# Sparse attention that feeds a feed-forward layer, one core: the first batch in another order with fewer instructions, and loads that wait for its first scores

## Chip, cores and metric

The kernel runs on one core of a Trainium2 chip. The metric is the time of one execution in device microseconds (us); the time given is the median of three runs. A page and a trace come from one further execution under the hardware profiler. The engines are named as the profile does: PE (TensorE matmul), PEld (its weight loads), DVE (VectorE), ACT (ScalarE), POOL (GpSimd) and SP (SyncE, which issues loads).

## What is computed

Eight batches of eight heads over 576 tokens with head size 64. The first four heads see the 32 newest keys, the other four the earlier keys of the same residue modulo 32. The heads side by side are the 4608 x 512 input of a feed-forward layer.

```python
scores = np.where(masks[None], scale * np.matmul(q, k.transpose(0, 1, 3, 2)), -1000000000.0)
attn = np.exp(scores - np.max(scores, axis=-1, keepdims=True))
attn = attn / (np.sum(attn, axis=-1, keepdims=True) + 1e-09)
x = np.matmul(attn, v).transpose(0, 2, 1, 3).reshape(B * S, H * D)
h = x @ w_in                                              # 512 -> 2048
g = np.where(h >= 1, h, np.where(h <= -1, 0.0, (h + 1) ** 2 / 4.0))
out = g @ w_out                                           # 2048 -> 512
```

## The kernel before

Attention of a batch is cut in four units: 0 and 1 hold the local heads, 2 and 3 the strided ones. A unit goes through small steps, each with a letter: `s` scores (PE, 96, 48, 48 and 40 small matmuls), the mask (`o` opens both banks with a zero matmul and `i` adds the mask on PE, then `X` and `S` take the maximum and subtract it on DVE straight from PSUM, or ACT copies the scores out with `g`; or `m` adds the mask on DVE), `x` maximum, `a`/`b` subtract, `e` exponential (ACT), `q` sum, `p` sum plus epsilon (ACT), `r` or `w` normalise (POOL or DVE), `f` transposes (PE), `c`/`d` copy them out (ACT, DVE), `v` values (PE), and `h`, `l` (`H`, `M` for tokens past 512) split the result into a rounded and a rest part, `xq_a` and `xq_b`. `0Zs0:17` is 17 zero matmuls into the bank that unit 0's scores will use; they compute nothing that is read.

The feed-forward layer multiplies split operands (three matmuls stand for one). The weights come as packed 64-bit words (`raw`) and are unpacked in five steps, `A` and `L` (ACT), `B` (DVE), `C` (POOL), `D` (ACT, or `g` on DVE) and `E` (DVE); `A0.1` is step A for block 0 of w_out. The first 512 tokens go through 16 up products `h_0` to `h_15`, of which `U` and `V` are the first two; each then has its down products. Later tokens run in larger groups until the end.

The order on every engine is the order in which the program issues, and that is written by hand: `AGENDA` lists the steps with a time in PE units, and the loops take from it what is due. All lines at -66.69 form the head of the program, ahead of the main loops. Loads go out on SP in program order. `load_w(0, 0, after)` makes ACT copy one element of `after` into the buffer of the first weights (`raw_0`), so SP issues that load, and all loads behind it, only after this copy; before, `after` is an element of `qk_1`, the second q and k load.

Of the kernel before, what the change touches and what calls it, by code (L numbers as in the profile page):

```python
# [28 lines left out]
-66.69 B0.1 L0.1  # L29
-63.035 A3.1 C0.1 A4.0 A1.1  # L30
-59.845 L3.0 C3.0 B1.1 D0.1 L1.1 C1.1 1m0 E0.1 1x0 1a0
-59.035 W6
-55.845 D3.0 E3.0 L5.0 L2.1 A5.0 B5.0 C5.0 B4.0
-54.19 L4.0 C4.0 D1.1 E1.1
-53.5 L3.1
-52.5 Z 1s1 1m1 B3.1
-51.845 L7.1 A2.1 B2.1 D4.0 E4.0
# [251 lines left out]
def tile_sparse_attention_then_ffn(  # L289
# [85 lines left out]

    ident_b = const.tile([P, P], BF16, name="ident_b")
    make_identity(nc, ident_b)
    zeros = const.tile([P, P], BF16, name="zeros")
    nc.vector.memset(zeros, 0.0)

# [102 lines left out]
    def whole(raw):  # L483
        return raw[:, :, 1].bitcast(F32).rearrange("p (h e) -> p h e", e=HF)
# [4 lines left out]
        for raw, to in words(f, i):  # L489
            copy(to[:, :, 0], whole(raw))  # L490

    def conv_e(f, i):
        for raw, to in words(f, i):
            nc.vector.tensor_tensor(out=to[:, :, 1], in0=whole(raw), in1=to[:, :, 0].bitcast(F32), op=ALU.subtract)

    def blocks(i, j):
        return wt[i, j].bitcast(F32).rearrange("p a b x e -> p (a b) x e")
# [28 lines left out]
    def ship_sums(i, j):  # L526
        nc.scalar.dma_start(kept[i][j][1], sums.pop((i, j)))

    loaded = {}

    def load_qk(b, p):
        src = qk_l[b, p] if p < 2 else qk_s[b, p - 2]
# [38 lines left out]
    def attention(b, kinds):  # L571
# [2 lines left out]

            return b > 1 and u == 0

        probs, flipped, there, ahead, covered = {}, {}, {}, {}, set()

        def banks(u, kind):

# [11 lines left out]
        def zero(u, kind, n):  # L592
# [4 lines left out]
            N = min(t.shape[1], 256)  # L597
            for _ in range(n):
                nc.tensor.matmul(t[:, :N], zeros, zeros[:, :1].broadcast_to([P, N]), start=True, stop=True)

        def score(u, pairs=range(2)):
            local, b0, nb = UNITS[u]
            Q, W, I, p0 = (QL, WL, IL, 0) if local else (QS, WS, IS, 2)
            if 0 in pairs:
                probs[u] = banks(u, "s"), W
            sc = probs[u][0]
            for p in pairs:
                qk_of = loaded[b, p0 + p, "qk"]
                for n in range(nb):
                    q0 = (b0 + n) * (QL if local else WS)  # L610
                    k0 = qk_of.shape[2] + (q0 - ST if local else q0)
                    for j in range(2):
                        _, s, i = seat(u, n, j)
                        if wide(u):
                            i = n % 2 * 2 + n // 2 % 2
                        qk = qk_of[j * D:(j + 1) * D].rearrange("d t s -> d (t s)")
                        nc.tensor.matmul(sc[j][i * Q:(i + 1) * Q, s, p], qk[:, q0:q0 + Q],  # L617
                                         qk[:, k0:k0 + W], start=u not in covered,
                                         stop=u not in covered)

        def score_0(u):
            score(u, (0,))
# [284 lines left out]
        def in_two(do, rest):  # L907

            return lambda u: do(u, rest if b == 0 else None)

        steps = {"s": score, "y": score_0, "z": score_1, "m": mask, "o": opened, "i": cover, "g": plain, "X": most_there, "S": below_there, "x": most, "w": norm_v, "a": below_max, "e": expo, "q": total, "p": plus_eps, "k": plus_eps_v, "b": below_max_v, "r": norm,
                 "f": flip, "t": turn, "j": spread, "J": gather, "c": keep, "d": keep_v, "v": value, "V": values_1_3, "h": in_two(high, False), "l": in_two(low, False), "H": in_two(high, True), "M": in_two(low, True),
                 "Q": lambda p: fetch_qk(b, p), "P": lambda n: last_weights(n), "F": lambda n: fetch_v(b, ((0, 0), (0, 1), (1, 0), (2, 0), (3, 0))[n])}
        def go(names):
            for name in names.split():
                if name[0] == "Z":
                    zero(int(name[2]), name[1], int(name[4:]))
                    continue
                steps[name[0]](int(name[1]))

# [2 lines left out]

    o_ps, outs = {}, {}

    def up(c, f, first=True, last=True):
# [7 lines left out]
        if not (first and last):  # L934
# [240 lines left out]
    def down_block(s, between):  # L1175
        home = {"y": ("b0", "b1"), "x": ("b2", "b3"), "z": ("b2", "b3")}
        for n, (m, k) in enumerate(DOWN):
# [14 lines left out]
                fetch_w(done - 2 + jj + WR)  # L1192
            between(n)

    FREE = {"s0": "oo", "s1": "aa", "s2": "hh", "s3": "oo", "f0": "oo", "f1": "hh", "f2": "oo", "f3": "oo",
            "v0": "aa", "v1": "hh", "v2": "oo", "v3": "aa"}
    first = attention(0, lambda u, kind: FREE[kind + str(u)][0])
# [18 lines left out]
    with tc.manual_schedule():
        for p in range(4):
            load_qk(0, p)
        load_w(0, 0, loaded[0, 1, "qk"][0:1, 0, 0:1])
# [22 lines left out]
        def step(name):  # L1242

            kind, rest = name[0], name[1:]
            if kind.isdigit():
                goes[int(kind)](rest)
            elif kind == "G":
                s, what, m, k = rest
                if what in "sr":
                    (prep if what == "s" else result)(int(s), int(m), int(k))  # L1250
                else:
                    g_sum(int(m), int(k), nc.vector if what == "t" else nc.gpsimd)
            elif kind == "X":
# [129 lines left out]
```

## Time and profile before

| what | value |
|---|---|
| median of three runs | 802.72 us (801.84 to 802.77) |
| the profiled execution | 803.35 us, of which the span of the trace is 801.2 us |
| PE busy | 791.7 us, 99% of the span |
| DVE, ACT, POOL busy | 618.7, 503.6, 259.6 us |
| data moved by DMA | 208.67 MB, mean 260 GB/s |

The profiled execution is 0.63 us above the median. Matmuls are pipelined, so a row of PE can overlap the next; the distance from start to start is what one costs when they follow each other.

### The profile page before, as it was taken

Reading aid. Unit: us, or ns where it says so; the run is one execution under the profiler, and the core shown is the slowest. Engines: PE = TensorE matmul, PEld = TensorE weight load, DVE = VectorE, ACT = ScalarE, POOL = GpSimd, SP = SyncE. Lnnn points to the kernel's source line nnn. Section 1 sums busy time; section 2 is a strip of 40 time slices with the busy share of each in tenths; the row PEclk is TensorE's granted clock in tenths of the full one; section 3 lists DMA queues with packets and bytes.
Section 4 is the critical chain, followed back from the end, with each engine's and each line's share of the span. In section 5 each row is a group of like instructions: output and inputs, shape, how many; then the busy total and the mean of one; then the engine's idle time right before and its main releaser. Section 6 shows DMA issues by size and latency. Waiting matters only on the chain.

```text
span 801.2 us, 17214 instructions
## 1 busy us (share of the span) xinstructions
PE 791.7 (99%) x6641; PEld 646.5 (81%) x6641; DVE 618.7 (77%) x855; ACT 503.6 (63%) x854; POOL 259.6 (32%) x202
## 2 busy tenths in 40 slices
PE   8999999999999999999999999999999999999998
PEld 5778888878888888878888888888888888888886
DVE  4899979898989999978679786675786854566673
ACT  4899764566764555677665455778544667775442
POOL 4466325897674320022141102132424001224000
PEclk9999999999999999999999999999999999999999
DMA  9967878998899999898789778777787676666765
GB/s 345 390 218 250 334 259 291 300 295 301 268 335 315 293 304 349 271 292 272 240 255 305 232 224 262 240 230 225 214 263 238 210 243 195 190 195 188 221 199 167
DMA packets 106224, 208.67 MB, mean 260 GB/s; under 512 B 17696, under 2 KB 30496, under 8 KB 104096
## 3 DMA queue, kind: packets, MB, share of 16 engines
q1 hardware_dynamic: 99088, 178.09, 69.3%
q10 hardware_dynamic: 7056, 29.49, 9.9%
q8 instruction: 53, 0.87, 0.5%
q14 instruction: 27, 0.22, 0.1%
HBM read 160.76 MB, written 46.78 MB: 259 GB/s over the span
## 4 chain that ended last, share of the span: by engine, by line
PE 87%; DVE 4%; DMA 4%; issue 1%; SPq 1%; POOL 1%; ACT 1%; ACTq 0%; DVEq 0%; POOLq 0%
PE yo L1188 22%; PE y L1093 16%; PE zo L1188 11%; PE h L940 9%; PE z L1093 8%; PE xo L1188 5%; PE o L1000 5%; PE x L1093 4%; PE sc L617 3%; PE xp L832 2%; DMA qk<-in_qk_s 1%; DMA v_w<-in_v_w 1%; DMA windows<-t 1%; PE xp L820 1%; DVE st L524 1%
## 5 line engine op out<-in xcount | busy, mean ns | idle before, releaser
L1188 PE MATMUL yo<-hl,wr 128*128 128x512 f32 x768 | 177.6, 390 | 0.0
L1188 PEld LDWEIGHTS yo<-hl,wr 128*128 128x128 f32 x768 | 143.6, 188 | 30.8 <-DVE hl L1050 0.9
L1093 PE MATMUL y<-x,wr 128*128 128x512 f32 x576 | 139.9, 390 | 0.0
L1093 PEld LDWEIGHTS y<-x,wr 128*128 128x128 f32 x576 | 108.0, 188 | 22.5
L940 PE MATMUL h<-xq_a,w 128*128 128x512 f32 x384 | 123.3, 395 | 0.0
L1149 POOL TENSOR_TENSOR ga<-gb,ga 128x1024 f32<-128x1024 f32 x17 | 44.1, 2602 | 235.3 <-DVE ga L950 175.6
L1050 DVE TENSOR_TENSOR hl<-ga,hl 128x1024 fp32r<-128x1024 f32 x48 | 64.1, 1351 | 35.9 <-ACT hl L1049 35.8
L1188 PE MATMUL zo<-hl,wr 128*128 128x512 f32 x384 | 89.3, 391 | 0.0
L940 PEld LDWEIGHTS h<-xq_a,w 128*128 128x128 f32 x384 | 72.0, 188 | 16.3 <-DVE g L950 0.4
L1188 PEld LDWEIGHTS zo<-hl,wr 128*128 128x128 f32 x384 | 71.6, 188 | 15.6 <-DVE hl L1050 0.6
L1049 ACT CAST hl<-ga 128x1024 fp32r<-128x1024 f32 x48 | 49.9, 1050 | 50.9 <-PE yo L1188 16.5
L1093 PE MATMUL z<-x,wr 128*128 128x512 f32 x288 | 73.6, 391 | 0.3 <-DVE ga L1075 0.3
L940 PE MATMUL h<-xq_b,w 128*128 128x512 f32 x192 | 73.6, 391 | 0.1
L1093 PEld LDWEIGHTS z<-x,wr 128*128 128x128 f32 x288 | 53.7, 188 | 12.0 <-DVE ga L1075 0.8
L947 ACT ACTIVATE tmp<-tmp 128x512 f32<-128x512 f32 x96 | 60.8, 633 | 3.1
L1050 DVE TENSOR_TENSOR hl<-gb,hl 128x1024 fp32r<-128x1024 f32 x36 | 49.2, 1379 | 13.8 <-ACT hl L1049 13.7
L516 POOL TENSOR_TENSOR st<-st 128x256 f32<-128x256 f32 x48 | 52.8, 1102 | 15.0 <-DVE st L733 6.2
L1049 ACT CAST hl<-gb 128x1024 fp32r<-128x1024 f32 x36 | 37.7, 1056 | 31.3 <-PE zo L1188 15.3
L950 DVE SCALAR_TENSOR_TENSOR ga<-ga,tmp 128x512 f32<-128x512 f32 x48 | 33.0, 688 | 28.3 <-ACT tmp L947 28.1
L944 ACT ACTIVATE u<-h,half 128x512 f32<-128x512 f32 x48 | 32.9, 686 | 30.1 <-PE h L940 22.5
L481 POOL TENSOR_TENSOR raw<-raw 128x512 uint32<-128x512 uint32 (+1 forms) x33 | 35.4, 1082 | 43.1 <-DVE raw L477 15.5
L710 POOL TENSOR_TENSOR pr<-pr,st 128x384 f32<-128x384 f32 (+3 forms) x18 | 25.7, 1432 | 64.2 <-DVE st L706 64.0
(128 smaller groups left out, 1404.0 us busy)
## 6 DMA issues: line engine op xcount, KB each, us to landing
wr<-ks SPq DMA_DIRECT2D x224, 256.0 KB, 3.9
wr<-kq SPq DMA_DIRECT2D x168, 256.0 KB, 3.4
ks<-st ACTq DMA_DIRECT2D x16, 1024.0 KB, 5.7
raw<-in_w SPq DMA_DIRECT2D x31, 512.0 KB, 7.6
qk<-in_qk_s SPq DMA_DIRECT2D x16, 604.0 KB, 6.5
qk<-in_qk_l SPq DMA_DIRECT2D x16, 576.0 KB, 6.5
kq<-w ACTq DMA_DIRECT2D x16, 512.0 KB, 4.1
out<-kept SPq DMA_DIRECT2D x24, 256.0 KB, 3.8
```

The costliest lines, as they stand in the source:

```text
L481: nc.gpsimd.tensor_tensor(out=raw[:, :, 1], in0=raw[:, :, 1], in1=raw[:, :, 0], op=ALU.add)
L516: eng.tensor_tensor(out=st[:, to, 1], in0=st[:, x, 1], in1=st[:, y, 1], op=op)
L940: nc.tensor.matmul(o_ps[c, f], weight(f, 0, h)[:, x, e:e + P], xq[c][y][:, cc], start=first and n == 0, stop=last and n == len(todo) - 1)
L944: nc.scalar.activation(u, h, AF.Relu, bias=half, scale=0.5)
L947: nc.scalar.activation(u, u, AF.Square)
L950: nc.vector.scalar_tensor_tensor(out=to, in0=h, scalar=1.0, in1=u, op0=ALU.max, op1=ALU.min)
L1000: nc.tensor.matmul(o_ps["o"][d], weight(f, 1, h)[:, x, e:e + P], gs[y], start=f == 0 and n == 0, stop=f == NF - 1 and n == 2)
L1049: nc.scalar.copy(t[:, 0], src)
L1050: nc.vector.tensor_tensor(out=t[:, 1], in0=src, in1=t[:, 0].bitcast(F32), op=ALU.subtract)
L1093: nc.tensor.matmul(to, w_[:, a, c * P:(c + 1) * P], xc[m][:, b, c], start=m in (1, 2, 5) and c + q == 0, stop=c == 1 and q == 2, skip_grou ...
L1149: eng.tensor_tensor(out=to, in0=x, in1=y, op=op)
L1188: nc.tensor.matmul(to, w_[jj][:, a, d * P:(d + 1) * P], t[:, b, jj], start=m in (1, 2, 5) and k + jj + q == 0, stop=k == NP // 2 - 1 and j ...
```

## The change

In the head fewer PE instructions fill time: 17 bf16 zero matmuls of 256 columns become two f32 ones of 384 columns and two bf16 ones, and other fills are cut or dropped. Units 1 and 3 get their mask as the first write into the bank (`I`), and their scores add to it, so the zero matmul that opened the bank is gone. A matmul of 32 columns (`0T2`) writes a mark into unit 2's bank behind unit 0's scores; ACT's copy reads this mark instead of `qk_1`, so the loads behind q and k wait for unit 0's scores. `raw_2` is loaded ahead of `v_3`. The up product `U` is cut in three parts of 6, 4 and 2 matmuls instead of two, unit 2's values come ahead of it and unit 3's behind it; `V` follows the same parts. From the 21st up product on, results go round four banks instead of three. Some unpacking steps change place, and the gate of `h_0` (`H0`) stands in the agenda.

```diff
--66.69 0Zs0:17 0o0 0s0 0o1 0i0 0X0 0s1 0i1 0S0 0o3 0g1 0x1 0s2 0Zv0:3 0Zf0:3 0m2 0e0 0a1 A0.0 0s3 0i3 0e1 0x2 0q0
--66.69 0p0 0g3 0a2 0q1 0Zf0:9 0e2 0w0 0Zf0:5 0f0 0p1 0x3 0c0 B0.0 0v0 0b3 L0.0 0e3 0r1 0q2 0p2 0f1 C0.0 0r2 0q3
--66.69 A1.0 0d1 D0.0 0p3 0h0 0r3 L1.0 0l0 A2.0 0Zf2:4 0v1 B1.0 0f2 0h1 0d2 0f3 0c3 0Zv3:4 0v3 0l1 0H1 L2.0 C1.0 g1.0 0v2 E1.0
--66.69 0M1 0h3 B2.0 0l3 E0.0 0h2 0H3 C2.0 U0 0l2 g2.0 V0 0M3 U1 0H2 0M2 E2.0 V1 1F0 1F1 A3.0 1s0 A0.1 B3.0 W7
+-66.69 0Zs0:2 0Zs0:2b 0o0 0s0 0T2 I 0I1 0i0 0X0 0s1 0S0 0I3 0g1 0x1 0s2 0Zf0:1 0m2 0e0 0a1 A0.0 0s3 0e1 0x2 0q0
+-66.69 0p0 0g3 0a2 0q1 0e2 0w0 0Zf0:3 0Zf0:2b 0f0 0Zv0:2b 0p1 0x3 0c0 B0.0 0v0 0b3 L0.0 0e3 0r1 0q2 0p2 0f1 0Zv1:2b C0.0 0r2 0q3
+-66.69 A1.0 0d1 D0.0 0p3 0h0 0r3 L1.0 0l0 0v1 B1.0 0f2 0h1 A2.0 0d2 0f3 0c3 C1.0 0v2 0l1 g1.0 E0.0 B2.0 0h2
+-66.69 0l2 L2.0 C2.0 A0.1 U0 0v3 0h3 L0.1 E1.0 B0.1 C0.1 0l3 V0 0H3 0M3 g2.0 E2.0 U1 A3.0 U2 V1 V2 B3.0 H0 D0.1 0H1 0M1 E0.1 0H2 0M2 1F0 1F1 1s0 W7
...
+        def begun(u):
+
+            ahead[u, "s"] = ts = banks(u, "s")
+            nc.tensor.matmul(ts[0][:, 0, 0, :32], zeros, zeros[:, :1].broadcast_to([P, 32]), start=True, stop=True)
+            marks.append(ts[0][0:1, 0, 0, 0:1])
...
+            for t in ts:
+                nc.tensor.matmul(t, ident_b, m.broadcast_to([P, n, 2, W]), start=True, stop=True)
...
-            tag = ("b2", "b3") if NF * c + f < NF + 4 else ("b2", "b3", "b0")
+            tag = ("b2", "b3") if NF * c + f < NF + 4 else ("b0", "b1", "b2", "b3")
...
-            todo = [(cc, 0, y) for y in range(2) for cc in ((0, 1) if first else (2, 3))]
-            todo += [] if first else [(cc, 1, 0) for cc in range(NC)]
+            kinds_ = (((0, 0), (0, 1), (1, 0)), ((0, 0), (1, 0)), ((0, 1),))[part]
+            todo = [(cc, x, y) for x, y in kinds_ for cc in ((2, 3) if part else (0, 1))]
...
+    def first_loads():
+        load_w(0, 0, marks.pop())
         load_v(0, 0)
         load_v(0, 1)
         load_w(1, 0)
         load_v(0, 2)
+        load_w(2, 0)
         load_v(0, 3)
-        load_w(2, 0)
```

On ACT the first instruction behind the table load is the copy that holds back the loads. Before it reads a loaded tile:

```order
L447 ACT_TABLE_LOAD
L447 COPY raw_191<-qk_1_185 1x1
L676 COPY pr_1_333<-sc_1_0_291 128x128
L676 COPY pr_1_333<-sc_1_1_292 128x128
L676 COPY pr_1_333<-sc_1_0_291 64x128
```

On PE, in the changed kernel, the tile that this copy now reads (`sc_2_0`) is written behind the last of unit 0's scores and ahead of the masks of units 1 and 0:

```order
L618 MATMUL sc_0_0_191<-qk_1_185 32x64
L618 MATMUL sc_0_1_192<-qk_1_185 32x64
L638 LDWEIGHTS nothing
L638 MATMUL sc_2_0_247<-nothing 128x32
L650 LDWEIGHTS ident_b
L650 MATMUL sc_1_0_281<-m_loc,ident_b 128x256
```

So the copy moved from the arrival of `qk_1` to the end of unit 0's scores.

The second place on PE is the end of unit 2's scores (`sc_2`) and the start of unit 3's (`sc_3`). Before, six zero matmuls with their weight loads stand between them:

```order
L617 MATMUL sc_2_0_340<-qk_3_189 64x54
L617 MATMUL sc_2_1_341<-qk_3_189 64x54
L599 LDWEIGHTS zeros
L599 MATMUL xp_0_0_366<-zeros 128x256
...
L599 LDWEIGHTS zeros
L599 MATMUL tp_0_0_371<-zeros 128x256
L617 MATMUL sc_3_0_329<-qk_2_187 64x54
L617 MATMUL sc_3_1_330<-qk_2_187 64x54
```

Now there is one f32 zero matmul:

```order
L618 MATMUL sc_2_0_247<-qk_3_189 64x54
L618 MATMUL sc_2_1_248<-qk_3_189 64x54
L600 MATMUL tp_0_0_352<-nothing 128x384
L618 MATMUL sc_3_0_317<-qk_2_187 64x54
L618 MATMUL sc_3_1_318<-qk_2_187 64x54
```

With what stands ahead, unit 3's scores begin some 16 matmuls earlier in PE's program than before.

The third place on PE is the up products `h_0` (`U`) and `h_1` (`V`); `xp_2` and `xp_3` are the values of units 2 and 3. Before, both units' values come first:

```order
L832 MATMUL xp_2_1_615<-pT_2_568,v_2_None 64x64 x2
L940 MATMUL h_0_660<-xq_a,w_0_516 128x512 x2
L940 MATMUL h_0_660<-xq_b,w_0_516 128x512 x2
L940 MATMUL h_1_669<-xq_a,w_0_516 128x512 x2
L940 MATMUL h_1_669<-xq_b,w_0_516 128x512 x2
L940 MATMUL h_0_660<-xq_a,w_0_516 128x512 x2
```

Now six matmuls of `h_0`, which need units 0 and 1 alone, stand ahead of unit 3's values:

```order
L850 MATMUL xp_2_1_553<-pT_2_538,v_2_None 64x64 x2
L959 MATMUL h_0_590<-xq_a,w_0_492 128x512 x2
L959 MATMUL h_0_590<-xq_b,w_0_492 128x512 x2
L959 MATMUL h_0_590<-xq_a,w_0_492 128x512 x2
L850 MATMUL xp_3_0_597<-pT_3_548,v_3_263 64x64 x2
L850 MATMUL xp_3_1_598<-pT_3_548,v_3_263 64x64 x2
```

So the first part of `h_0` moved ahead of 40 small matmuls, and took the two matmuls with the weights' rest part along.

## Rows read from the trace of the kernel before

**Rows 1.** Waits of PE over the run: releaser, us in total, times, longest

```profile
PE tp L599 <- issue: 2.5, 1, 2.5
PE sc L599 <- DVE zeros L379: 1.0, 1, 1.0
PE xp L832 <- issue: 0.8, 1, 0.8
...
PE z L1093 <- DVE ga L1075: 0.3, 1, 0.3
```

**Rows 2.** Timeline of PE, 0 to 34 us: start, us from it, instruction, idle before

```profile
0.99 3.81 PE L599 MATMUL sc<-zeros 128*128 128x256 bf16 x17 [0.99 <-DVE zeros L379]
...
5.37 1.32 PE L617 MATMUL sc<-qk 64*32 64x64 f32 x96
...
8.57 0.98 PE L617 MATMUL sc<-qk 64*64 64x54 f32 x48
...
12.61 0.58 PE L599 MATMUL tp<-zeros 128*128 128x256 bf16 x2 [2.51 <-issue]
13.12 1.54 PE L617 MATMUL sc<-qk 64*64 64x54 f32 x40
...
15.11 2.15 PE L599 MATMUL tp<-zeros 128*128 128x256 bf16 x14
17.10 0.82 PE L747 MATMUL tp<-ident,pr 128*128 128x128 f32 x6
...
20.45 0.60 PE L599 MATMUL tp<-zeros 128*128 128x256 bf16 x4
...
25.44 0.46 PE L832 MATMUL xp<-pT,v 54*64 54x64 f32 x16 [0.78 <-issue]
...
26.53 0.73 PE L940 MATMUL h<-xq_a,w 128*128 128x512 f32 x2
...
28.03 0.62 PE L940 MATMUL h<-xq_b,w 128*128 128x512 f32 x2
28.48 0.61 PE L940 MATMUL h<-xq_a,w 128*128 128x512 f32 x2
...
32.80 1.17 PE L617 MATMUL sc<-qk 64*32 64x64 f32 x96
```

**Rows 3.** Page, sections 1 and 3: PE's instructions, packets of the instruction queue

```profile
PE 791.7 (99%) x6641; PEld 646.5 (81%) x6641; DVE 618.7 (77%) x855; ACT 503.6 (63%) x854; POOL 259.6 (32%) x202
...
q8 instruction: 53, 0.87, 0.5%
```

**Rows 4.** DMA of 10.0 to 10.5 us: queue, packets, MB, share

```profile
q8 instruction: 1, 0.02, 11.2%
```

**Rows 5.** Windows: busy time per engine (instructions), granted clock, DMA share, GB/s

```profile
4.00:8.00 4.00, 4.00 (x155) 2.67 (x154) 0.79 (x2) 0.19 (x1) 2.38 (x10) 1.00 1.00 408
...
12.00:14.00 2.00, 1.39 (x34) 0.98 (x35) 0.84 (x3) 1.17 (x3) 0.79 (x1) 0.65 1.01 409
14.00:16.00 2.00, 2.00 (x27) 1.41 (x20) 1.10 (x3) 0.90 (x4) 0.00 (x0) 0.50 1.01 408
...
45.00:60.00 15.00, 14.94 (x113) 12.12 (x112) 14.63 (x27) 14.94 (x26) 9.46 (x9) 1.00 0.79 282
```

**Rows 6.** Timeline of ACT, 5 to 16 us

```profile
5.79 0.19 ACT L447 COPY raw<-qk 1x1 f32<-1x1 f32 x1 [3.76 <-DMA qk<-in_qk_l]
...
12.35 0.66 ACT L469 ACTIVATE raw<-raw 128x512 f32<-128x512 f32 x1 [2.31 <-DMA raw<-in_w]
...
15.09 1.00 ACT L676 COPY pr<-sc 128x216 f32<-128x216 f32 x4 [1.57 <-PE sc L641]
```

**Rows 7.** Timeline of DVE, 14 to 21 us

```profile
14.17 0.96 DVE L734 TENSOR_TENSOR pr<-pr,st 128x768 f32<-128x768 f32 x1
...
20.54 0.62 DVE L757 COPY pT<-tp 128x256 f32<-128x256 f32 x2
```

**Rows 8.** Timeline of SP's queue, first load behind q and k

```profile
6.00 0.33 SPq L448 DMA_DIRECT2D raw<-in_w  x1
```

More of the change, by code (lines that the diff above doesn't have):

```diff
@@ L24 @@
 AGENDA = """
[L25 to L31 removed]
+-66.69 0Zs0:2 0Zs0:2b 0o0 0s0 0T2 I 0I1 0i0 0X0 0s1 0S0 0I3 0g1 0x1 0s2 0Zf0:1 0m2 0e0 0a1 A0.0 0s3 0e1 0x2 0q0
+-66.69 0p0 0g3 0a2 0q1 0e2 0w0 0Zf0:3 0Zf0:2b 0f0 0Zv0:2b 0p1 0x3 0c0 B0.0 0v0 0b3 L0.0 0e3 0r1 0q2 0p2 0f1 0Zv1:2b C0.0 0r2 0q3
+-66.69 A1.0 0d1 D0.0 0p3 0h0 0r3 L1.0 0l0 0v1 B1.0 0f2 0h1 A2.0 0d2 0f3 0c3 C1.0 0v2 0l1 g1.0 E0.0 B2.0 0h2
+-66.69 0l2 L2.0 C2.0 A0.1 U0 0v3 0h3 L0.1 E1.0 B0.1 C0.1 0l3 V0 0H3 0M3 g2.0 E2.0 U1 A3.0 U2 V1 V2 B3.0 H0 D0.1 0H1 0M1 E0.1 0H2 0M2 1F0 1F1 1s0 W7
+-63.035 A1.1 A3.1 A4.0
+-59.845 L3.0 C3.0 B1.1 L1.1 C1.1 1m0 1x0 1a0
 -59.035 W6
[L33 to L34 removed]
+-55.845 D3.0 E3.0 D1.1 L5.0 L2.1 A5.0 B5.0 C5.0 B4.0
+-55 E1.1
+-54.19 L4.0 C4.0
 -53.5 L3.1
[L36 to L37 removed]
+-52.5 Z 1s1 1m1
+-51.845 D4.0 E4.0 B3.1 L7.1 A2.1 B2.1
 -49.5 L6.0 A6.0 A4.1 C2.1 D2.1 E2.1 C3.1 D5.0 B6.0 C6.0 1e0 1q0
@@ L377, in tile_sparse_attention_then_ffn @@
     make_identity(nc, ident_b)
-    zeros = const.tile([P, P], BF16, name="zeros")
-    nc.vector.memset(zeros, 0.0)
+    nothing = const.tile([P, P], F32, name="nothing")
+    nc.vector.memset(nothing, 0.0)
+    zeros = nothing.bitcast(BF16)[:, :P]
     m_loc = const.tile([P, SLOTS, WL], BF16, name="m_loc")
@@ L490, in conv_d, with conv_e @@
             copy(to[:, :, 0], whole(raw))
-    def conv_e(f, i):
+    def conv_e(f, i, eng=nc.vector):
         for raw, to in words(f, i):
-            nc.vector.tensor_tensor(out=to[:, :, 1], in0=whole(raw), in1=to[:, :, 0].bitcast(F32), op=ALU.subtract)
+            eng.tensor_tensor(out=to[:, :, 1], in0=whole(raw), in1=to[:, :, 0].bitcast(F32), op=ALU.subtract)
     def blocks(i, j):
@@ L527, in ship_sums @@
         nc.scalar.dma_start(kept[i][j][1], sums.pop((i, j)))
-    loaded = {}
+    loaded, marks = {}, []
     def load_qk(b, p):
@@ L575, in wide @@
             return b > 1 and u == 0
-        probs, flipped, there, ahead, covered = {}, {}, {}, {}, set()
+        probs, flipped, there, ahead, covered, done_ = {}, {}, {}, {}, set(), set()
         def banks(u, kind):
@@ L590, in banks, with zero @@
             return [bank(tag, shape, f"{name}_{b}_{u}_{j}") for j, (tag, shape) in enumerate(zip(tags, shapes))]
-        def zero(u, kind, n):
+        def zero(u, kind, n, short_):
             ahead[u, kind] = ts = banks(u, kind)
@@ L596, in zero @@
             t = ts[0].rearrange(f"p {' '.join(names)} -> p ({' '.join(names)})")
-            N = min(t.shape[1], 256)
+            of = zeros if short_ else nothing
             for _ in range(n):
-                nc.tensor.matmul(t[:, :N], zeros, zeros[:, :1].broadcast_to([P, N]), start=True, stop=True)
+                nc.tensor.matmul(t, of, of[:, :1].broadcast_to(list(t.shape)), start=True, stop=True)
         def score(u, pairs=range(2)):
@@ L618, in score @@
                                          qk[:, k0:k0 + W], start=u not in covered,
-                                         stop=u not in covered)
+                                         stop=u not in covered or u in done_, skip_group_check=u in done_)
         def score_0(u):
@@ L632, in opened, with masked @@
                 nc.tensor.matmul(t, zeros, zeros[:, :1].unsqueeze(1).unsqueeze(1).broadcast_to(list(t.shape)), start=True, stop=False)
+        def begun(u):
+            ahead[u, "s"] = ts = banks(u, "s")
+            nc.tensor.matmul(ts[0][:, 0, 0, :32], zeros, zeros[:, :1].broadcast_to([P, 32]), start=True, stop=True)
+            marks.append(ts[0][0:1, 0, 0, 0:1])
+        def masked(u):
+            local, b0, _ = UNITS[u]
+            ahead[u, "s"] = ts = banks(u, "s")
+            covered.add(u)
+            done_.add(u)
+            n, W = slots(u)[0], WL if local else WS
+            m = m_loc[:, b0 and 1:][:, :n].unsqueeze(2) if local else m_str.unsqueeze(1).unsqueeze(1)
+            for t in ts:
+                nc.tensor.matmul(t, ident_b, m.broadcast_to([P, n, 2, W]), start=True, stop=True)
         def cover(u):
@@ L909, in in_two @@
             return lambda u: do(u, rest if b == 0 else None)
-        steps = {"s": score, "y": score_0, "z": score_1, "m": mask, "o": opened, "i": cover, "g": plain, "X": most_there, "S": below_there, "x": most, "w": norm_v, "a": below_max, "e": expo, "q": total, "p": plus_eps, "k": plus_eps_v, "b": below_max_v, "r": norm,
+        steps = {"s": score, "y": score_0, "z": score_1, "m": mask, "o": opened, "I": masked, "T": begun, "i": cover, "g": plain, "X": most_there, "S": below_there, "x": most, "w": norm_v, "a": below_max, "e": expo, "q": total, "p": plus_eps, "k": plus_eps_v, "b": below_max_v, "r": norm,
                  "f": flip, "t": turn, "j": spread, "J": gather, "c": keep, "d": keep_v, "v": value, "V": values_1_3, "h": in_two(high, False), "l": in_two(low, False), "H": in_two(high, True), "M": in_two(low, True),
@@ L916, in go @@
                 if name[0] == "Z":
-                    zero(int(name[2]), name[1], int(name[4:]))
+                    zero(int(name[2]), name[1], int(name[4]), name[5:] == "b")
                     continue
@@ L924, in tile_sparse_attention_then_ffn, with up @@
     o_ps, outs = {}, {}
-    def up(c, f, first=True, last=True):
+    def up(c, f, part=None):
+        first, last = part in (None, 0), part in (None, 2)
         if first:
-            tag = ("b2", "b3") if NF * c + f < NF + 4 else ("b2", "b3", "b0")
+            tag = ("b2", "b3") if NF * c + f < NF + 4 else ("b0", "b1", "b2", "b3")
             o_ps[c, f] = bank(tag[(NF * c + f) % len(tag)], [P, CH], f"h_{c}_{f}")
@@ L933, in up @@
             todo.sort(key=lambda n: n[2])
-        if not (first and last):
-            todo = [(cc, 0, y) for y in range(2) for cc in ((0, 1) if first else (2, 3))]
-            todo += [] if first else [(cc, 1, 0) for cc in range(NC)]
+        if part is not None:
+            kinds_ = (((0, 0), (0, 1), (1, 0)), ((0, 0), (1, 0)), ((0, 1),))[part]
+            todo = [(cc, x, y) for x, y in kinds_ for cc in ((2, 3) if part else (0, 1))]
         for n, (cc, x, y) in enumerate(todo):
@@ L1193, in down_block @@
             between(n)
-    FREE = {"s0": "oo", "s1": "aa", "s2": "hh", "s3": "oo", "f0": "oo", "f1": "hh", "f2": "oo", "f3": "oo",
-            "v0": "aa", "v1": "hh", "v2": "oo", "v3": "aa"}
-    first = attention(0, lambda u, kind: FREE[kind + str(u)][0])
+    B01, B45 = ("b0", "b1"), ("b4", "b5")
+    FREE = {"s0": "o", "s1": "a", "s2": "h", "s3": "o", "f0": B01, "f1": "h", "f2": B01, "f3": "h",
+            "v0": "a", "v1": B45, "v2": B01, "v3": "a"}
+    first = attention(0, lambda u, kind: FREE[kind + str(u)])
     MORE = set("2s2 2v0 2v1 3s0 3s2 3v1 4s0 4s1 4v0 5s0 5s2 5v1 5v2 6s3 7s0 7s1 7v0 7v1".split())
@@ L1204, in tile_sparse_attention_then_ffn @@
     conv = {"A": conv_a, "L": conv_l, "B": conv_b, "C": conv_c, "D": conv_d, "E": conv_e,
-            "g": lambda f, i: conv_d(f, i, nc.vector.tensor_copy)}
+            "g": lambda f, i: conv_d(f, i, nc.vector.tensor_copy), "f": lambda f, i: conv_e(f, i, nc.gpsimd)}
     def last_weights(n):
@@ L1214, in last_weights @@
                 load_piece(NF - 1, 0, k, o_p, "ob", 2)
[L1216 to L1219, printed above, removed]
+    def first_loads():
+        load_w(0, 0, marks.pop())
         load_v(0, 0)
@@ L1234, in tile_sparse_attention_then_ffn @@
                 load_w(f, i)
+    with tc.manual_schedule():
+        for p in range(4):
+            load_qk(0, p)
         goes = {b: attention(b, room(b)) if b else first for b in range(B)}
@@ L1254, in step @@
                 x_step(*map(int, rest.split(".")))
+            elif name == "H0":
+                gate(0)
             elif kind in "UV":
-                up(0, int(kind == "V"), rest == "0", rest == "1")
+                up(0, int(kind == "V"), int(rest))
+            elif kind == "I":
+                first_loads()
             elif kind == "Z":
@@ L1294, in tile_sparse_attention_then_ffn @@
                 up(0, f)
-            todo = [(GATE, lambda: gate(f)), (ROUNDED, lambda: pend.append((f, rounded(f))))]
+            todo = [(GATE, lambda: gate(f))] if f else []
+            todo += [(ROUNDED, lambda: pend.append((f, rounded(f))))]
             if f > 1:
```

## The prediction

> **What bounds the kernel now.** I read the page first: PE is busy for 791.7 of 801.2 us [rows 3], so a gain can only come from time in which PE waits or does work that nothing reads. The list of PE's waits [rows 1] says where that is: 3.3 us lie in two waits for "issue", one of 2.51 us that ends at 12.61 and one of 0.78 us that ends at 25.44 [rows 2], and 1.0 before the first instruction; of its seven rows no other reaches that. So I read the timeline of PE's first 34 us [rows 2]. Behind 34 us PE is dense, and what the head gains or loses moves all that follows.
>
> In the head PE comes to 12.61, does unit 3's scores from 13.12 to about 14.6, then 14 zero matmuls from 15.11 to about 17.1, and unit 0's transposes at 17.10. [...] The transposes need unit 0's normalised probabilities, which DVE finishes at 14.17 + 0.96 = 15.13 [rows 7]. So for 2 us PE was late by its own doing: the wait, the lower clock and the zero matmuls queued ahead.
>
> What is that wait? "Issue" means that no semaphore ended it. Two facts point to the program itself being fetched. The page has 53 packets with 0.87 MB on an instruction queue, 16 KB each, and PE has 6641 matmuls and as many weight loads, 13282 in all [rows 3]: 251 per packet. And between the two stalls PE issues 254 matmuls (the counts of the timeline's rows from 12.61 up to the one at 25.44, added), 508 instructions with their loads, about two packets. One packet of that queue runs within 10.0 to 10.5 us [rows 4], and PE goes on some 2.3 us later. The block before ended 256 instructions earlier, in unit 0's scores (5.37 to about 6.6 [rows 2]), at about 6.3. So the packet waited some 4 us for its turn, while the DMA engines were at a share of 1.00 [rows 5] with q, k and the first weights, whose load was issued at 6.00 [rows 8].
>
> **The change, part by part.** The profiled execution is 803.35 us, of which 2.15 lie outside the span; sums are made against it, and the median of the runs shown lies 0.63 lower.
>
> *First fetch.* 17 fills go, as do two pairs of zero matmuls that opened banks, and five of six fills between units 2 and 3. An f32 matmul counts as two (96 in the trace for 48 in the program). Before unit 3's scores PE then has 209 matmuls where it had 225, so the boundary that lay ahead of these scores now falls some 15 matmuls into them: it moves by about 0.5 us in PE's time. More counts that raw_0 and what is behind it are issued only after unit 0's scores, about 6.5 plus a copy of 0.19 [rows 6] and the issue, some 7.05. The fetch asked for at about 6.3 then finds only the rest of q and k ahead of it, and these are in by about 9 at the latest, since unit 2's scores run on them from 8.57 without a wait [rows 2]. So I put the packet at 8.3 and its use 2.3 later, 10.6. PE gets there at about 10.1: 0.5 us of stall in place of 2.51, and no reason for the lower clock. Ends: none of it (the packet as late as before) and all of it.
>
> *Unit 0's transposes.* With PE early, DVE's normalising decides. It ends 2.78 us after the step A0.0 starts on ACT (12.35 to 15.13 [rows 6, 7]), and A0.0 waited 2.31 us for raw_0. This load goes out 1.05 us later, but up to 8 us the DMA engines are busy anyway, at a share of 1.00 [rows 5], with q and k, and the fetch that ran in raw_0's midst is out of its way. I take raw_0 0.2 us earlier: normalised at 14.9, transposes at 15.0, gain 2.1. Ends: the whole 1.05 us arrives (16.2, gain 0.9), or raw_0 gains 0.8 (14.4, gain 2.7). What is queued behind A0.0 on ACT (e1, p0) and waits for it on DVE (q1, w0) is in this 2.78.
>
> *Price of the f32 fills.* The trace has none. Its bf16 fill of 256 columns takes 3.81/17 = 0.22 us at the start [rows 2], so one of 384 columns 0.34; an f32 one takes at least that, at the most four such passes, 1.34 us. I take the upper end, as f32 transposes of 128 columns take 0.14 each [rows 2] at full clock and are slower than bf16 by column. At the start 2 x 1.34 + 2 x 0.34, and 0.68 for the two matmuls that open the banks, make 4.0 us, so unit 0's scores begin at 5.0 to 5.4: no loss against 5.37. The three behind unit 3's scores cost up to 2.2 us at full clock, 11.5 to 13.7: hidden under the normalising until 15.0. [...]
>
> *Dropped fills later.* Four at 20.45 cost 0.60 [rows 2], four more before unit 3's values, of the same kind, as much; two short pairs come in, about 0.6 together. Unit 1's values wait for DVE's copy at 20.54 [rows 7] in any case. Ends 0 and 0.6; I take 0.3.
>
> *Second fetch.* The DMA share is as high, and the boundary lies near the first part of U. I leave its 0.78 us as it is (ends: 0.5 more, or gone).
>
> *U and V in three parts.* From 26.53 to 32.80 stand 24 matmuls; a pair takes 0.45 where they follow each other (28.03 to 28.48 [rows 2]), 5.4 in all. 0.87 us is waiting for units 2 and 3. The new order puts six matmuls ahead of 40 small ones that wait for unit 3: ends 0 and 0.87, I take 0.4.
>
> *Nothing from:* four banks, since no wait of PE behind 34 us is for one (cover: PE's dense run; without it some 0.3 us, the wait of z for DVE [rows 1]); the mark (32 columns); masks as first write, whose inputs POOL has ready; raw_2 ahead of v_3, by some 1 us, which is long there when unit 3's values stall at 25.44.
>
> *Sum at batch 1's scores:* 2.1 + 0.3 + 0 + 0.4 = 2.8, so 30.0 for 32.80.
>
> *Given back.* From 45 to 60 us ACT is busy 14.94 and DVE 14.63 of 15 us [rows 5]: PE's lead holds only if they too are early. They are, mostly: ACT loses its idle 1.57 us before 15.09 [rows 6]. I let 0.3 be eaten (ends 0 and 2.0). Lasting gain 2.5: profiled 800.85, median 800.2.
>
> [...]
>
> **The rivals.**
>
> *As late.* The stall is not a fetch, or it starts as late as before. PE resumes at about 12.55 with 25 of 40 score matmuls left, at half clock until 13.5; then two f32 fills at 1.34 fill the time to 16.1, the rest runs to 17.1. Transposes as before; 0.7 from the later parts, 0.3 given back: 802.3. For it: the second boundary in between did not stall PE at all, so I can't tell what makes one late. Against: the bytes ahead of the fetch are fewer.
>
> *Loads late.* raw_0 lands the whole 1.05 later, gain 0.9 + 0.7, of which 0.3 are given back: 1.3, so 801.4. For it: A0.0 waited for this load alone. Against: engines at a share of 1.00 lose no time by a later issue.
>
> *Eaten.* The weights of the next products come no earlier, since loads are bound by DMA until 36 us, and ACT and DVE have no room up to 60: 2.0 of 2.8 go, 801.9. For it: 14.94 of 15 us. Against: their waits in the head shrink too.
>
> *Slower: the clock.* With few fills PE is idle from the end of Zf0 (12.4 to 13.7) to 15.0. If the granted clock falls to 0.50 there, as it did behind 2.51 us of idle, the transposes and values run at half speed. For the 3.4 us for which it stayed low before that costs at most 1.7 of the gain. It decides the sign from 5 us at half speed on (half of it is lost, 2.5); if it holds until U and V run dense, from 13.5 to 22 and more, it loses half of 8.5, 4.3: 1.8 slower, 804.5. For it: the fills that filled 14 of these waits are gone. Against: before, the clock came back by 16 us with no denser work.
>
> [...]
>
> **How the numbers follow.** A change of under 0.2%, 1.6 us, is about what a measurement of this kernel can't tell from none. Chances: the forecast (799.0 to 801.1) 0.52; as late 0.17; loads late 0.13; eaten 0.11; the clock 0.07. Loads late and eaten lie near the bound of 801.1; I count 0.04 of each as faster, the rest as the same, and the forecast wholly as faster: 0.60 faster, 0.33 same, 0.07 slower. The prediction is the likeliest, 800.2. The range reaches up to 803.2, past as late with 0.9 for its bounds, and leaves out the clock; down to 798.4, a gain of 4.3, short of all good ends at once (2.7 + 0.6 + 0.78 + 0.87 = 4.95).
>
> **What would show it.** Right: no "issue" wait over 1 us before 15 us; the instruction packet near 8.3; the granted clock 1.00 in 12 to 16; unit 0's transposes at 14.4 to 15.5, released by DVE; U's first matmul near 23 and batch 1's scores at 29.5 to 30.5; A0.0 at about 12.1. Wrong: a wait of over 2 us ahead of or within unit 3's scores (as late); A0.0 at 13 or later (loads late); batch 1's scores at 30 but a gain under 1 at 60 us, with waits of PE for ACT or DVE (eaten); a stretch at 0.50 (the clock).

## Result and profile after

The changed kernel takes 806.26 us (804.58 to 810.05, nine runs) against 802.69 us for the kernel before (801.15 to 803.46, nine runs): 1.0053 times as long, 95% interval 1.0036 to 1.0071. It is 0.5% slower, where 2.5 us of gain were forecast, and lies outside the range. Its profiled execution took 808.78 us, of which 806.9 are the span.

PE's waits in it (releaser, us in total, times, longest) answer to [rows 1]:

```profile
PE tp L765 <- DVE pr L752: 2.0, 1, 2.0
PE sc L618 <- DMA qk<-in_qk_s: 1.7, 3, 0.8
PE xp L850 <- issue: 1.2, 1, 1.2
...
PE y L1112 <- DMA wr<-ks: 0.8, 1, 0.8
PE o L1019 <- ACT w L491: 0.7, 1, 0.7
```

The wait of 2.51 us for issue is gone, as forecast. In its place PE waits 2.0 us for DVE. The others come later: o at 51, sc (batch 1's q and k, 1.4 of its 1.7 us) at 61 and 62, xp at 169 and y at 542 us; the kernel before waits at none of these places for more than 0.3 us. The timeline of PE's head answers to [rows 2]:

```profile
10.91 0.92 PE L618 MATMUL sc<-qk 64*64 64x54 f32 x40
11.76 2.54 PE L600 MATMUL tp<-nothing 128*128 128x384 f32 x8
16.31 0.84 PE L765 MATMUL tp<-ident,pr 128*128 128x128 f32 x6 [2.01 <-DVE pr L752]
...
27.35 1.01 PE L959 MATMUL h<-xq_a,w 128*128 128x512 f32 x2
...
34.28 1.17 PE L618 MATMUL sc<-qk 64*32 64x64 f32 x96
```

Unit 3's scores run through, 2.2 us earlier than in [rows 2]. The transposes come only 0.8 us earlier, U begins 0.8 us later, and batch 1's scores 1.5 us later. The windows (columns as in [rows 5]) show why:

```profile
14.00:16.00 2.00, 0.30 (x2) 0.00 (x0) 1.48 (x3) 1.94 (x8) 0.00 (x0) 1.00 1.00 392
16.00:20.00 4.00, 3.62 (x94) 3.21 (x98) 3.36 (x8) 3.27 (x9) 2.06 (x3) 0.72 1.04 420
20.00:24.00 4.00, 4.00 (x78) 3.45 (x72) 2.20 (x6) 2.58 (x8) 2.54 (x3) 0.50 1.03 412
24.00:28.00 4.00, 4.00 (x60) 3.45 (x59) 2.78 (x7) 1.78 (x5) 0.59 (x1) 0.50 1.01 407
```

PE stands still for 2 us, and then the granted clock is 0.50 nearly up to 28 us. ACT and SP show the start of it:

```profile
13.39 0.65 ACT L470 ACTIVATE raw<-raw 128x512 f32<-128x512 f32 x1 [2.99 <-DMA raw<-in_w]
```

```profile
7.35 0.33 SPq L449 DMA_DIRECT2D raw<-in_w  x1
```

The first weights are issued 1.35 us later than in [rows 8] and unpacked 1.04 us later than in [rows 6].

That is one execution. Its clock over the whole run was 0.993; of the nine, two had under 0.997 (808.78 and 810.05 us) and seven 0.999 or 1.000, with a median of 805.96. So the head's low clock does not explain the whole result: full-clock runs lose 3 us as well.

### The profile page after: what moved, and what is told of

It reads as the page before. It is cut to its first block, busy times and chain, and to the rows that moved or that the text cites. A ratio compares the mean times of both kernels' runs of the same rounds, so it can differ in the third digit from the quotient of the medians.

```text
span 806.9 us, 17164 instructions
## 1 busy us (share of the span) xinstructions
PE 794.2 (98%) x6613; PEld 646.9 (80%) x6613; DVE 619.0 (77%) x855; ACT 504.6 (63%) x854; POOL 259.5 (32%) x202
## 4 chain that ended last, share of the span: by engine, by line
PE 87%; DMA 5%; DVE 3%; ACT 2%; SPq 1%; POOL 1%; issue 1%; DVEq 0%; POOLq 0%
PE yo L1207 21%; PE y L1112 15%; PE h L959 13%; PE zo L1207 11%; PE z L1112 8%; PE xo L1207 5%; PE x L1112 4%; PE o L1019 3%; PE xp L850 3%; PE sc L618 2%; DMA wr<-ks 1%; DMA qk<-in_qk_s 1%; PE xp L838 1%; DMA raw<-in_w 1%; DMA wr<-kq 1%; PE tp L765 1%
```

## Experiments

Each kernel is compared with the kernel before, run on the same chip in the same series; the medians of the kernel before were 802.25 to 802.58 us. "Low" counts executions whose mean granted clock is below 0.997; the kernel before has 1 such in 106.

| kernel | median us | ratio to before, 95% interval | low |
|---|---|---|---|
| after_again | 809.08 | 1.0071 (1.0048 to 1.0094) | 7 of 10 |
| gate_qk | 805.77 | 1.0039 (1.0021 to 1.0057) | 2 of 10 |
| new_head | 806.08 | 1.0041 (1.0014 to 1.0069) | 5 of 10 |
| old_head | 803.11 | 1.0011 (0.9993 to 1.0028) | 0 of 10 |
| align | 803.47 | 1.0014 (0.9995 to 1.0033) | 1 of 10 |
| align_bridge | 803.95 | 1.0013 (0.9997 to 1.0030) | 0 of 10 |
| align_gate | 803.57 | 1.0011 (0.9994 to 1.0027) | 0 of 10 |
| before_minus | 806.71 | 1.0043 (1.0024 to 1.0063) | 1 of 10 |
| minus_padded | 802.60 | 0.9998 (0.9985 to 1.0012) | 0 of 10 |
| before_plus26 | 804.75 | 1.0032 (1.0017 to 1.0047) | 1 of 10 |
| before_plus38 | 808.33 | 1.0070 (1.0043 to 1.0096) | 3 of 4 |
| pad_start | 804.23 | 1.0025 (1.0008 to 1.0043) | 2 of 10 |
| mark_old | 804.68 | 1.0028 (1.0011 to 1.0044) | 3 of 10 |
| u3_oldconv | 803.73 | 1.0019 (0.9999 to 1.0039) | 1 of 10 |

**after_again**, the changed kernel, no edit. 

> The changed kernel once more. In its profile PE waited 2.0 us for unit 0's normalising, then the granted clock was 0.50 for 10.2 us, and batch 1's scores began 1.48 us late; 2.5 us more were lost between 43 and 60 us, 0.9 at 169 us in a wait for issue and 1.3 near 540 us for a load. Theory 1 (the low clock behind the wait is most of the loss): a run that keeps the full clock begins batch 1's scores at 30.5 to 32.5 and takes 802 to 804. Theory 2 (the later loads and the order of the unpacking cost the rest): such a run still takes 804.5 to 806.5, with ACT and DVE waiting in 34 to 62 us.

Its profile has the full clock (803.97 us, span 802.2). Two rows of PE's timeline and its waits:

```profile
14.83 0.85 PE L765 MATMUL tp<-ident,pr 128*128 128x128 f32 x6 [0.94 <-DVE pr L752]
...
29.66 1.23 PE L618 MATMUL sc<-qk 64*32 64x64 f32 x96
```

```profile
PE xp L850 <- issue: 1.3, 1, 1.3
...
PE z L1112 <- DMA wr<-ks: 0.9, 1, 0.9
PE sc L618 <- DMA qk<-in_qk_s: 0.8, 1, 0.8
PE o L1019 <- ACT w L491: 0.7, 1, 0.7
PE y L1112 <- DMA wr<-ks: 0.4, 1, 0.4
```

Batch 1's scores begin 4.6 us earlier than in the low-clock profile: 1.5 us of that are there when the transposes begin, from the later weights of that execution, and 3.1 come behind them, with the low clock. Low executions are 9 of 19. With 29.66 even the sum at batch 1's scores is reached (30.0 forecast). But the run ends 1.6 us behind the median of the kernel before. Theory 1 is right for the head, and the 803.97 us of this one execution lie in its range too; but of the ten full-clock runs of both series nine take 804.58 to 807.39, so most of the loss lies elsewhere, and theory 2 holds for its times, not yet for its causes.

**before_again**, the kernel before, no edit. 

> The kernel before, for a second profile. Its runs on this chip show a granted clock of 1.000 in about half and 0.997 to 0.998 in a third, the latter some 1.8 us longer. If the wait of 2.51 us for issue ahead of unit 3's scores (and the half clock behind it) comes only in some executions, a profile at 1.000 has no such wait, begins batch 1's scores at 30 to 31 instead of 32.8, and takes 801 to 802.3. If it comes in every execution, the wait is here again.

800.82 us, span 798.7, clock 1.000. PE's timeline:

```profile
10.71 0.38 PE L599 MATMUL tp<-zeros 128*128 128x256 bf16 x2 [0.53 <-issue]
...
14.38 0.85 PE L747 MATMUL tp<-ident,pr 128*128 128x128 f32 x6 [0.50 <-DVE pr L734]
...
23.63 0.46 PE L832 MATMUL xp<-pT,v 54*64 54x64 f32 x16 [1.50 <-issue]
...
30.94 1.17 PE L617 MATMUL sc<-qk 64*32 64x64 f32 x96
```

The wait that carried the forecast is 0.53 us here, no low clock follows, and the transposes stand at 14.38, before the 15.0 forecast for the changed kernel. In the first 31 comparison runs of the kernel before, 22 have a clock of 0.999 or 1.000 (median 801.96), nine a lower one (803.62). The profile shown was of the second kind.

I matched the two full-clock profiles, after_again and before_again, matmul by matmul. At 34 us after_again is 1.2 us ahead, at the end 3.5 us behind. It loses 1.3 us at 46 to 48 us (PE's wait for ACT's `w`), 0.95 at 54 to 58 (the wait for batch 1's q and k), 1.0 at 164 (xp) and 1.8 at 533 to 540 (the waits for `wr`), and gains 0.4 at 233. None of these waits lies at a boundary between blocks of 256 instructions (13588 of PE for the 53 packets of [rows 3]; new_head below shows a wait at a boundary).

**gate_qk**: loads wait for `qk_1` again.

```diff
-0s0 0T2 I 0I1
+0s0 0I1
-        load_w(0, 0, marks.pop())
+        load_w(0, 0, loaded[0, 1, "qk"][0:1, 0, 0:1])
```

> The changed kernel, but its loads wait for the second q and k load as before; no mark. If the later loads are the cause: the first weights land 1 us earlier (step A0.0 at 12.0 to 12.5), transposes at 15.0 to 15.4, idle time ahead of them under 1.2 us, full clock, and 800 to 803. If the order behind the head is the cause: the head gains the same, but 2 us or more are lost between 43 and 60 us and it takes 803.5 to 805.5. If the fetch needs the later loads, a wait for issue of over 1 us comes back ahead of 15 us.

A0.0 starts at 11.28, the transposes at 14.30, both 0.7 us ahead of what was expected, and batch 1's scores at 29.09 are earlier than in after_again. Still it takes 805.77 us: the time is not lost in the head of this profile, and against before_again 2.3 us are lost between 44 and 58 us.

**new_head** and **old_head**: the changed kernel with one half of the steps taken from the kernel before.

```diff
 new_head: lines 1 and 2 of the agenda (without 0Zv1:2b), the gate and raw_2 ahead of v_3 of after; rest, up(), FREE and three banks of before
 old_head: lines 1 and 2 of the agenda and the gate of before; rest, up(), FREE and four banks of after
```

> The changed kernel's first two lines of steps (fewer fills, masks first, mark, later loads), and the kernel before for the rest: up products in two parts, old order of unpacking, three banks. If the head is the cause: 803.5 to 806, with the wait ahead of the transposes and a low clock in some runs. If what comes behind is the cause: 800 to 802.

> The first two lines of steps and the loads' gate of the kernel before, and the changed kernel for the rest: up products in three parts, new order of unpacking, four banks, raw_2 ahead of v_3. If the rest is the cause: 804 to 806, with ACT or DVE waiting in 34 to 62 us. If the head is: 801.5 to 803.5.

The loss goes with the head's lines, though no profile shows it in the head alone. new_head's timeline has a wait of 3.20 us that I take for a fetch: this matmul stands exactly 256 instructions behind instruction 449 of PE, at which the kernel before waits 2.51 us in [rows 2], 1.47 us of them behind the end of the packet that ran from 10.25 to 11.14. A place 256 instructions or a multiple of that from there I call a boundary.

```profile
21.68 0.42 PE L851 MATMUL xp<-pT,v 64*64 64x32 f32 x12 [3.20 <-issue]
```

old_head holds U and V in three parts, four banks, the new unpacking order and raw_2 ahead of v_3: together they move nothing that can be measured. That they bring nothing was not the forecast (0.7 from the first). Its profile shows why: it is 0.95 us ahead of before_again at batch 1's scores, and loses 1.25 us at 46 to 48 us.

**align**, **align_bridge**, **align_gate**: what the head's lines change behind the head is the place of every later boundary between blocks of 256 instructions. PE runs 13536 instructions in the changed kernel and 13588 before; these three have 13584 to 13587.

```diff
-0Zs0:2 0Zs0:2b ... 0Zf0:1 ... 0Zf0:3 0Zf0:2b
+0Zs0:12c       ... 0Zf0:8c ... 0Zf0:22c
 c: bf16, 256 columns; align_bridge: 0Zf0:22b (384 columns); align_gate: align with the gate of gate_qk
```

> The changed kernel with its f32 fills replaced by 42 bf16 fills of 256 columns (12 at the start, 8 ahead of unit 3's scores, 22 ahead of the transposes) of about the same length, so that PE has 52 instructions more and all later 256-instruction boundaries stand where the kernel before has them. If fewer instructions cost time by moving the fetches onto SP's issues (the loads near 530 us late by 1.4 to 1.8 us in four profiles of the changed head, each with a fetch within 0.3 us of a slow issue), that loss is gone and the full-clock runs take 802 to 803.5; low-clock runs stay as frequent as in the changed kernel. If the boundaries don't matter: 804 to 805.5 at full clock, with the loss at 530 us.

> As align, but the 22 fills ahead of the transposes have 384 columns, so that PE is busy about 1.2 us longer there; the same number of instructions. If PE's idle time ahead of the transposes is what lowers the clock: runs with a mean clock below 0.997 become rare (0 to 2 of 10, against 9 of 19 so far), and the median is 3 us or more under that of align if align has many of them. If the clock falls for another reason: as many as in align.

> As align, with the loads waiting for the second q and k load as before. If later loads and moved boundaries are the two costs of the new head, both are gone: 801.5 to 803 and hardly a low-clock run. If the order behind the head costs as well (2 us between 43 and 60 us in two profiles), it stays at 802.5 to 804.

With some 52 instructions more the loss shrinks from 3.4 to 6.7 us (gate_qk, after_again) to 1.2 to 1.6, and can no longer be told from none. The three hardly differ: with the boundaries back, ten runs each show no effect of the gate or the bridge. Low runs did not stay as frequent as align's expectation had it: 1 of 10. In align's profile the waits for xp and `wr` are gone; the 1.2 us at 46 to 48 us are not, though there it has no lead on before_again:

```profile
PE o L1020 <- ACT w L491: 0.7, 1, 0.7
```

**before_minus**: only the fills change.

```diff
-0Zs0:17 ... 0Zv0:3 0Zf0:3 ... 0Zf0:9 0e2 0w0 0Zf0:5 ... 0Zf2:4 ... 0Zv3:4
+0Zs0:2 0Zs0:2b ... 0Zf0:1 ... 0Zf0:3 0e2 0w0 0Zf0:2b ... 0Zv3:3c
```

> The kernel before with nothing changed but its fills: 26 fewer zero matmuls (52 instructions fewer with their loads), f32 ones in place of most bf16 ones, so that from the transposes on the boundaries of 256 instructions stand where the changed kernel has them. If moved boundaries cost time by themselves: 804 to 806, with waits for late loads or gathers at 165 to 190 or near 530 us that the kernel before does not have. If not: 801.5 to 803.

The whole loss, 4.1 us, without any other part of the change. Its profile shows a stall far from the head, exactly at a boundary; over it PE falls back 2.3 us, half of the 4.6 by which this profile ends behind before_again:

```profile
226.55 0.73 PE L959 MATMUL h<-xq_a,w 128*128 128x512 f32 x2 [2.11 <-issue]
```

**minus_padded**, **before_plus26**, **before_plus38**: the place or the number?

```diff
 minus_padded:  before_minus with 0Zs0:2 -> 0Zs0:30n (n: bf16, 64 columns)
 before_plus26: before with 0Zs0:17 -> 0Zs0:43n (n: bf16, 100 columns)
 before_plus38: before_plus26 with 0Zf0:9 -> 0Zf0:17n, 0Zf0:5 -> 0Zf0:9n
```

> before_minus (806.7 against 802.6) with its 52 missing instructions put back at the very start, as 30 narrow zero matmuls in place of two f32 ones; all later fills stay as few as in before_minus. If the place of the boundaries is the cause, the loss is gone: 802 to 803.5. If the missing fills themselves cost it (PE's clock or its lead), it stays at 805 to 807.

> The kernel before with 26 zero matmuls more at the start (43 of 100 columns for 17 of 256, about as long), so 52 instructions more and every later boundary 52 instructions earlier in the work. If it is the place of the boundaries that counts, and the kernel before stands in a good place: slower, 803.5 to 807. If fewer instructions as such cost: 801.5 to 802.7.

> As before_plus26 with 12 fills more ahead of the transposes (26 of 100 columns for 14 of 256): 76 instructions more than the kernel before. The same two expectations; a time apart from before_plus26's by more than 1.5 us shows that the place counts and not the number.

By instructions against the kernel before: -52 is 806.7, 0 (put back at the start) 802.6, +52 804.75, +76 808.33. It is the place: fewer cost as more do, and neither the missing fills nor the f32 ones behind the start, which minus_padded keeps, cost anything. before_plus38's timeline and windows show the worst case, a boundary inside scores of a later batch, and the clock behind it; the two together put PE 5.6 us back:

```profile
302.24 0.57 PE L617 MATMUL sc<-qk 64*64 64x54 f32 x10 [2.48 <-issue]
```

```profile
300.00:304.00 4.00, 1.76 (x13) 1.47 (x13) 3.81 (x4) 1.69 (x8) 0.00 (x0) 0.70 0.98 362
304.00:308.00 4.00, 4.00 (x10) 3.06 (x10) 0.00 (x0) 0.00 (x0) 0.00 (x0) 0.50 0.20 74
```

**pad_start** (f32 fills kept, boundaries as before), **mark_old** (old_head with the mark), **u3_oldconv** (align_gate with the old unpacking order).

```diff
 pad_start:  after with 0Zs0:2 -> 0Zs0:30n (n: bf16, 64 columns)
 mark_old:   old_head with 0s0 -> 0s0 0T2 I, load_w(0, 0, marks.pop())
 u3_oldconv: align_gate with A0.1 to E0.1 and all lines from -63.035 to -51.845 of before
```

> The changed kernel with its f32 fills kept ahead of the transposes and its two f32 fills at the very start replaced by 30 narrow bf16 ones: 52 instructions more, boundaries as in the kernel before. Theory a (moved boundaries): full-clock runs 802 to 803.7 as in align, no loss near 530 us. Theory b (f32 fills ahead of the transposes don't hold the clock up): low-clock runs (below 0.997) in 3 or more of 10, at 806 or more. If low clock came from where the boundaries lie, at most 1 or 2 of 10 are low.

> old_head (803.1, none of 10 runs below 0.997) with the one thing added that its loads wait for the mark behind unit 0's scores. If later loads cost time in themselves: A0.0 1 us later, PE's wait ahead of the transposes 1 us longer, median 804 to 806 with low-clock runs. If they cost nothing as long as the fills stay: 802.5 to 803.8.

> align_gate (803.6) with the unpacking order of the kernel before from batch 1's scores on; U and V stay in three parts, masks first, four banks. If the new unpacking order loses the 1.4 to 1.6 us between 43 and 60 us: 801.8 to 802.8, no wait of PE for ACT in 40 to 60 us. If that loss comes from the three parts of U and V or from a lead that ACT can't follow: 803 to 804.

pad_start takes 2 to 5 us off the changed kernel's time and keeps two low runs: boundaries confirmed, the fills' type not settled (2 of 10 against 1 of 10 in align). mark_old puts 1.6 us and three low runs on old_head, but the two intervals overlap. Both have the mark, and both stay above 1 with their intervals, so boundaries may not be all of it. In u3_oldconv ACT no longer waits in 34 to 60 us, and still it is no faster than align_gate. The loss at 46 to 48 us is gone from its profile, but 1.7 us are lost between 34 and 42, with three short waits of PE for `w`: the unpacking order decides where the time is lost, and this swap does not save it.

## Why the prediction was wrong

**The step that failed** is "Nothing from" together with "Second fetch": I looked at two of some 53 boundaries, and priced moving the rest at nothing. before_minus shows what it costs alone: 4.1 us, as much as the whole change (3.6 and 6.7 us in its two series), and it is undone by putting 52 instructions back (minus_padded). What the runs showed in its place is that the price hangs on where the boundaries fall: 806.7 us with 52 instructions fewer, 802.6 with as many as before, 804.75 and 808.33 with 52 and 76 more. In part it is PE's own stall: 2.1 us at one boundary in before_minus. In the profiles of the changed kernel no wait of PE lies at a boundary; there the waits for `wr` (1.8 us in after_again), which align does not have, are the part that can be put down to a moved fetch, by way of SP (below).

**Unit 0's transposes** (gain 2.1): mis-sized by the execution that I took as typical. That the wait was a fetch is borne out: in the profile before a packet ends at 11.14 us and another at 23.94, and PE's two waits for issue end 1.47 and 1.50 us later. In the profile after the packet ends at 9.12 us, and the wait ahead of unit 3's scores, at 10.91, is gone. The packet came when forecast: in the profile after, the DMA of 8.0 to 8.5 us has

```profile
q8 instruction: 1, 0.02, 11.9%
```

for 8.3. But that was luck: the later loads did not bring it there. before_again, whose loads go out as before, has the same line for 8.0 to 8.5 us, and in all profiles but the one shown before the packet runs at 8.0 to 8.8 us, with the mark or without it; in that one it ran at 10.25. By the clocks of its runs, most executions of the kernel before are of before_again's kind and wait little there. Against before_again the transposes come 0.45 us (after_again) to 1.9 us (after) late. That the profiled execution stood 0.63 us above the median was written beside the table, and its low clock, 0.65 and 0.50, stood in [rows 5].

**Price of the f32 fills.** The sum has a slip: at 1.34 us each, the three behind unit 3's scores and the two bf16 ones come to 4.7 us at full clock, not 2.2, and would have stood in front of the transposes. The row at 11.76 us in the profile after has 2.54 us for them at full clock, from start to start 0.65 for an f32 fill and 0.16 for a bf16 one of the same 384 columns: the four passes of the sum's upper end, but of a bf16 fill that takes half the 0.34 us that the sum had. So the cover held.

**Loads late** was a rival at 0.13 and came true in the middle of the profiles: in the seven with the mark A0.0 starts at 11.6 to 13.4, middle 12.4, without it at 11.3 to 12.0 (12.35 in the one shown before), middle 11.4. The 1.0 us between them is about the whole delay of the load (1.05 in the forecast). The step that "engines at a share of 1.00 lose no time by a later issue" failed.

**The clock** was priced somewhat high and given too small a chance: 4.3 us forecast, 3.1 measured from the transposes to batch 1's scores between the two profiles of the changed kernel, in 9 of 19 runs instead of 0.07. Low runs go with the mark and with the moved boundaries, and most with both: 14 of 29 with both (after, after_again, new_head), 6 of 40 with the mark alone (align, align_bridge, pad_start, mark_old), 3 of 20 with about 52 instructions fewer alone (gate_qk, before_minus), 1 of 40 with neither; the two kernels with more instructions than before are left out. A clock of 0.50 came behind 2.01 us of idle in after (for DVE), and behind 3.20 us in new_head and 2.48 us in before_plus38 (both for issue); but behind the 2.11 us in before_minus, whose clock over the run is 1.000, matmuls follow 0.23 us apart as they did ahead of it, so the wait alone does not decide it.

**Given back** (0.3) was 2.1: after_again leads before_again by 1.28 us at batch 1's scores, yet unit 2's scores of batch 1, at 55.9 in both, run on in the one and wait 0.81 us in the other. ACT has hardly any room there; the kernel before uses nearly all of it, and the changed one loses 1.1 us of it. before_again's windows, and ACT's wait in 34 to 60 us in after_again:

```profile
40.00:45.00 5.00, 5.00 (x23) 3.86 (x22) 4.86 (x12) 4.97 (x10) 2.72 (x4) 1.00 0.23 55
45.00:50.00 5.00, 5.00 (x24) 4.14 (x23) 4.91 (x11) 4.97 (x9) 2.03 (x2) 1.00 0.84 270
```

```profile
ACT w L491 <- POOL raw L482: 1.1, 1, 1.1
```

So **eaten** came true by its size, but only in part as it was meant. All nine profiles with the new unpacking order lose about 1.25 us at 46 to 48 us, align's too, which has no lead to lose; new_head, with the old order, loses none there. This is a price of the new order, on which the prediction puts no term. A lead is eaten as well: before_minus, with the old order, is 1.1 us ahead of before_again at 40 us and 0.2 at 60. Four banks and the mask as first write brought nothing visible, as forecast; they were not run alone.

**The blocks.** The prediction's 256 instructions a block, where [rows 3] gave it 251, are what the traces show: PE's 13588 instructions, semaphore ones included, make 256 for each of the 53 packets in [rows 3], and the stalls of 3.20, 2.11 and 2.48 us stand at multiples of 256 behind instruction 449. In the profiles of before and after the packets keep step with PE: the first ends 1.5 and 2.0 us ahead of instruction 449, and each of the next 51 starts less than 512 instructions ahead of its own place, 256 further on each time, and ends before PE is there. Few boundaries cost PE a wait: of some 53, PE waits more than 0.3 us for issue at 2 in before_again, 2 in before_minus, 3 in before_plus38 and none in after_again. The costs that these profiles show are such waits, of 0.5 to 3.2 us, and the slow issues on SP beside a packet (2.61 us for 0.91, below).

**Left open:** which runs turn low and why only half; what PE's wait for xp at 164 to 169 us is, which is for issue and not at a boundary, and which mark_old has too; and how the moved boundaries' price divides in the median between PE's own stall and the way by SP (below), since each kernel has one profile or two.

## What to carry to other kernels

Here 52 PE instructions fewer moved the later boundaries and cost 4.1 us (before_minus), and with 52 put back the loss was gone (minus_padded, 802.60 us): before crediting or blaming a change in the number of instructions, pad it to the old count and time that too. Take the wait that a forecast rests on from more than one execution (2.51 us in one, 0.53 in the next), above all if the profiled one is slower than the median or its clock is lower. Ask what the next full engine can follow: a lead of 1.28 us at batch 1's scores was gone at 55.9 us, with ACT busy for 4.97 of 5 us from 45 to 50 us; and a new order can cost behind the head what it gains in front, here 1.25 us at 46 to 48 us.

## What the hardware showed beyond that

A fetch of PE's also went with held-up loads of another engine. SP's queue in before_again and in after_again, the same two transfers:

```profile
527.58 0.91 SPq L780 DMA_DIRECT2D windows<-t  x2
```

```profile
529.26 2.61 SPq L798 DMA_DIRECT2D windows<-t  x2
```

and the DMA of 529.2 to 529.7 us in after_again:

```profile
q8 instruction: 1, 0.02, 20.6%
```

SP issues these two in 2.61 us, with PE's packet beside them, instead of 0.91; the loads behind go out later, and PE then waits 0.9 and 0.4 us for `wr`. The same two issues take 1.9 to 2.4 us in the profiles of after, gate_qk, new_head and before_minus, each with a packet of PE's at their side, and 0.91 in the two of before and in old_head. In six more profiles the packet runs beside an earlier issue of the same group: that one is then slow, 0.63 us in align_gate and 1.13 in minus_padded where it takes 0.42 without a packet, and PE waits at most 0.3 us for `wr`. So the slow issue goes where the packet goes; no run moved this one packet alone. That 52 or 76 of PE's 13588 instructions more or less change the time by 0.3 to 0.7% was the surprise of this study.
